# BigBird attention and MLP-mixer on one Trainium2 core: head pairs with row-tiled score matmuls, long row loads, token mixing in half batches, instructions ordered by hand

## The chip, the cores and the metric

The kernel runs on one core of one Trainium2 chip. The time is device time in microseconds (us), the median of the fast runs. Runs that fell in a slower state are left out: one of the kernel before (1022.83 us).

PE is the matmul engine, DVE the vector engine, ACT the scalar engine, POOL the engine that issues the loads here. PSUM tiles are where PE leaves its results; in both kernels the mixer has two of them (the pool named `psM`, tiles named `pm`). QK is the score matmul, PV the product of the exponentials with the values; tok1, tok2, ch1 and ch2 are the four matmul stages of the mixer. A link is a step that the next one must wait for, such as a group of matmuls or the operation that empties its tile. "L362" is line 362 of the kernel in question. "Granted clock" is the share of full speed that PE was given; 0.5 is the half clock. Its record begins with its first change, so the head of the span shows 1.00 even where matmuls took twice as long.

## The reference

Four batches, 8 heads, 768 positions, head size 64. Block-sparse attention (24 blocks of 32, a mask from band, edges and three sampled blocks per row) is followed by an MLP-mixer over the 512 channels:

```python
mask = (np.abs(blk_i - blk_j) <= 1) | first_or_last_block | sampled        # 768 x 768
scores = np.where(mask, q @ k.T / 8, -1e9);  attn = softmax(scores);  x = attn @ v
x = x.transpose(0, 2, 1, 3).reshape(4, 768, 512)
h = np.maximum(x.T @ w_tok1, 0.0) @ w_tok2          # token mixing: 768 -> 256 -> 768
u = x + h.T
out = u + np.maximum(u @ w_ch1, 0.0) @ w_ch2        # channel mixing: 512 -> 1536 -> 512
```

## The kernel before

It computes every score (the mask doesn't save work), transposed: keys on the partitions. One head is a slot; the mask rides in 24 extra rows of the operands, so that one 88-row matmul gives masked scores. The mixer of a batch runs beside the attention of the next. The order is left to a scheduler with priorities.

```python
def qkv_src_ap(t, b, h):                                  # 256-byte pieces (64 floats)
    return APx(t, (b * H + h) * S * D, [[D, 128], [128 * D, NC], [1, D]])
# ... per slot: 6 transposes of q and of k, each 64 wide (qtb, ktb rows 0..63); rows 64..87 hold the mask
for j in range(NC):                                       # NC = 6 key blocks of 128
    ps = psS.tile([128, S], FP32, tag="ps", ...)
    nc.tensor.matmul(out=ps[:, 0:512], lhsT=kt[0:88, 128*j:128*j+128], rhs=qt[0:88, 0:512], ...)
    nc.tensor.matmul(out=ps[:, 512:768], lhsT=kt[0:88, 128*j:128*j+128], rhs=qt[0:88, 512:768], ...)
    nc.scalar.activation(out=et[:, j, :], in_=ps[:, :], func=AF.Exp, scale=0.125)
    for c in range(NC):                                   # PV, 65 columns (64 + the row sum)
        nc.tensor.matmul(out=po[:, c, :], lhsT=et[:, j, 128*c:128*c+128], rhs=vaug[n][:, j, :], ...)
# ... the mixer of a whole batch: 2 groups tok1, 6 tok2 (+ transposes of u), 24 ch1, 6 ch2
# ... every group: matmuls into a pm tile (two of them), then a DVE operation that empties it
```

The softmax here doesn't subtract the row's maximum and nothing guards it: scores larger than these inputs give would overflow.

## Time and profile before

364.21 us in the median, with 2786 matmuls. The prediction below shows the busy table, the stages and the order on PE; what it leaves out is the clock in 40 slices of the span, the DMA packets by size, and two groups of instructions (busy us, mean ns of one, then idle time before them and its cause).

ACT does the exponentials alone, and the mixer's ReLUs lie on DVE.

### The profile page before, as it was taken

The numbers are of one execution on the slowest core, as the hardware profiler recorded it, in microseconds if no ns is written. First come the engines' busy times: TensorE is split into PE (matmuls) and PEld (weight loads), VectorE is DVE, ScalarE is ACT, GpSimd is POOL, SyncE is SP. The second block draws the span as 40 slices with busy tenths as digits, with TensorE's granted clock in tenths as the row PEclk, the third lists the DMA queues.
The fourth block names the chain that finished last, engine by engine and source line by source line (L and its number), as shares of the span: only waits on it lengthen the run. The fifth ranks groups of instructions, "written<-read, shape, count | busy, mean of one in ns | idle before, by whom it ended". The sixth has DMA issues, their size and how long they took to land.

```text
span 362.9 us, 6617 instructions
## 1 busy us (share of the span) xinstructions
PE 325.2 (90%) x2786; PEld 183.3 (51%) x2786; DVE 182.1 (50%) x478; ACT 142.1 (39%) x193; POOL 89.7 (25%) x123
## 2 busy tenths in 40 slices
PE   0795688899899999999999999999999999679995
PEld 0453356565556555455555555455555555235542
DVE  3331243436768633356667544347676534546722
ACT  1293467775622334465604333385404440000000
POOL 9954543524310222233210222220000000000000
PEclk9997599999999999999999999999999999859999
DMA  5999959688641455559531565651101012000022
GB/s 40 136 198 194 153 37 67 46 54 53 41 29 8 28 62 85 84 61 60 33 23 11 34 88 84 75 51 12 13 0 13 2 58 98 21 0 2 0 85 90
DMA packets 82162, 20.24 MB, mean 56 GB/s; under 512 B 75892, under 2 KB 78548, under 8 KB 82132
## 3 DMA queue, kind: packets, MB, share of 16 engines
q0 software_dynamic: 78496, 13.38, 47.3%
q1 hardware_dynamic: 3636, 6.44, 4.7%
q8 instruction: 22, 0.36, 0.4%
q14 instruction: 8, 0.07, 0.1%
HBM read 26.74 MB, written 6.29 MB: 91 GB/s over the span
## 4 chain that ended last, share of the span: by engine, by line
PE 76%; ACT 8%; DMA 8%; POOL 3%; DVE 2%; issue 2%; ACTq 0%; POOLq 0%
PE pm_ch L296 19%; PE pm_ch L313 16%; PE ps L214 13%; PE po L224 10%; ACT et L222 8%; PE ps L218 5%; PE tk L196 4%; DMA w_ch<-in_moe_w_ch_dram 3%; PE pm_tok L249 3%; PE tq L188 3%; PE pm_tok L268 3%; DMA qsrc<-in_q_dram 3%; DMA w_tok<-in_moe_w_tok_dram 2%; PE pm_ut L279 2%; DVE u L276 1%
## 5 line engine op out<-in xcount | busy, mean ns | idle before, releaser
L222 ACT ACTIVATE et<-ps 128x768 bf16<-128x768 f32 x192 | 140.8, 814 | 155.2 <-PE po L224 132.6
L214 PE MATMUL ps<-qtb,ktb 88*128 88x512 bf16 x192 | 76.3, 397 | 7.8 <-ACT et L222 6.4
L296 PE MATMUL pm_ch<-uT,w_ch 128*128 128x384 bf16 x384 | 75.0, 332 | 0.0
L313 PE MATMUL pm_ch<-w_ch,rc 128*128 128x512 bf16 x288 | 71.4, 379 | 0.0
L302 DVE TENSOR_SCALAR rc<-pm_ch 128x384 bf16<-128x384 f32 x96 | 53.1, 556 | 18.3 <-PE pm_ch L296 14.3
L224 PEld LDWEIGHTS <-et 128*128 128x128 bf16 x1152 | 50.7, 100 | 18.0 <-issue 2.8
L224 PE MATMUL po<-vaug,et 128*128 128x65 bf16 x1152 | 58.2, 196 | 0.0
L218 PE MATMUL ps<-qtb,ktb 88*128 88x256 bf16 x192 | 54.2, 282 | 0.0
L132 POOL DMA_DIRECT2D ksrc<-in_k_dram x32 | 26.7, 833 | 96.1 <-PE tk L196 86.0
L296 PEld LDWEIGHTS <-w_ch 128*128 128x128 bf16 x384 | 36.7, 99 | 27.1 <-issue 4.2
L193 DVE COPY qtb<-tq 64x768 bf16<-64x768 bf16 x32 | 17.6, 549 | 61.3 <-PE ps L218 59.7
L134 POOL DMA_DIRECT2D vaug<-in_v_dram x32 | 26.5, 829 | 77.6 <-PE po L224 74.3
L313 PEld LDWEIGHTS <-rc 128*128 128x128 bf16 x288 | 26.5, 97 | 27.5
L234 DVE TENSOR_SCALAR x<-po,recip 128x64 bf16<-128x64 f32 x192 | 39.7, 276 | 1.0
L320 DVE TENSOR_TENSOR o<-pm_ch,u 128x512 f32<-128x512 f32 x24 | 16.5, 687 | 38.7 <-PE pm_ch L313 38.7
L201 DVE COPY ktb<-tk 64x768 bf16<-64x768 bf16 x32 | 17.6, 549 | 34.6 <-PE tk L196 32.5
L218 PEld LDWEIGHTS <-ktb 88*128 88x128 bf16 x192 | 19.0, 99 | 27.3 <-issue 19.3
L133 POOL DMA_DIRECT2D qsrc<-in_q_dram x32 | 26.6, 831 | 8.5 <-PE tq L188 7.8
L214 PEld LDWEIGHTS <-ktb 88*128 88x128 bf16 x192 | 19.0, 99 | 14.1 <-issue 2.8
L188 PE MATMUL tq<-ident,qsrc 128*64 128x128 bf16 x192 | 18.3, 236 | 7.6 <-DMA qsrc<-in_q_dram 5.9
L196 PE MATMUL tk<-ident,ksrc 128*64 128x128 bf16 x192 | 23.0, 234 | 1.1 <-DVE qtb L193 1.1
L196 PEld LDWEIGHTS <-ksrc 128*64 128x64 bf16 x192 | 13.5, 113 | 18.3 <-issue 17.3
(48 smaller groups left out, 127.5 us busy)
## 6 DMA issues: line engine op xcount, KB each, us to landing
out_dram<-o SPq DMA_DIRECT2D x24, 256.0 KB, 2.3
ksrc<-in_k_dram POOLq DMA_DIRECT2D x32, 96.0 KB, 3.1
qsrc<-in_q_dram POOLq DMA_DIRECT2D x32, 96.0 KB, 3.4
vaug<-in_v_dram POOLq DMA_DIRECT2D x32, 96.0 KB, 3.1
w_ch<-in_moe_w_ch_dram POOLq DMA_DIRECT2D x8, 384.0 KB, 11.1
w_tok<-in_moe_w_tok_dram POOLq DMA_DIRECT2D x2, 384.0 KB, 7.3
ktb<-indf SPq DMA_DIRECT2D x2, 36.0 KB
qtb<-e2sb SPq DMA_DIRECT2D x2, 36.0 KB
```

Of the source, the lines that this page charges most:

```text
L132: nc.gpsimd.dma_start(out=ksrc[n][:, :, :], in_=qkv_src_ap(k, b, h))
L133: nc.gpsimd.dma_start(out=qsrc[n][:, :, :], in_=qkv_src_ap(q, b, h))
L188: nc.tensor.matmul(out=tq[:, 128 * c : 128 * c + 128], lhsT=qsrc[n][:, c, :], rhs=ident[:, :], start=(c == 0), stop=(c == NC - 1), is_tran ...
L196: nc.tensor.matmul(out=tk[:, 128 * c : 128 * c + 128], lhsT=ksrc[n][:, c, :], rhs=ident[:, :], start=(c == 0), stop=(c == NC - 1), is_tran ...
L214: nc.tensor.matmul(out=ps[:, 0:512], lhsT=kt[0:88, 128 * j : 128 * j + 128], rhs=qt[0:88, 0:512], start=True, stop=True,)
L218: nc.tensor.matmul(out=ps[:, 512:768], lhsT=kt[0:88, 128 * j : 128 * j + 128], rhs=qt[0:88, 512:768], start=True, stop=True,)
L222: nc.scalar.activation(out=et[:, j, :], in_=ps[:, :], func=AF.Exp, scale=0.125)
L224: nc.tensor.matmul(out=po[:, c, :], lhsT=et[:, j, 128 * c : 128 * c + 128], rhs=vaug[n][:, j, :], start=(j == 0 and c == 0), stop=(j == NC ...
L234: nc.vector.tensor_scalar(out=x_tiles[c][:, 64 * h : 64 * h + 64], in0=po[:, c, 0:64], scalar1=recip[:, c : c + 1], scalar2=None, op0=ALU. ...
L296: nc.tensor.matmul(out=pm[:, 0:384], lhsT=w_ch1[:, dmc, 128 * cc : 128 * cc + 128], rhs=st["uT"][:, dmc, 384 * sh : 384 * sh + 384], start ...
L302: nc.vector.tensor_scalar(out=rc[:, cc, 384 * sh : 384 * sh + 384], in0=pm[:, 0:384], scalar1=0.0, scalar2=None, op0=ALU.max,)
L313: nc.tensor.matmul(out=pm[:, :], lhsT=rc[:, cc, 128 * sc : 128 * sc + 128], rhs=w_ch2[:, cc, :], start=(cc == 0), stop=(cc == 11),)
```

## The change

Its intent, part by part: two heads share the array as row tiles (64 rows each), so that their score matmuls may run side by side; the mask, which has no rows left, comes by a second row-tiled pair of matmuls; positions are permuted so that a partition loads 1.5 KB in one row; token mixing is done in two channel halves, the first as soon as two of the four head pairs of a batch are there; and every engine's order is written by hand, with generators that yield the PE nanoseconds of each matmul. The diff replaces nearly the whole body. Its core:

```diff
-    for j in range(NC):                       # one head, 88 rows, mask included
-        nc.tensor.matmul(out=ps[:, 0:512],   lhsT=kt[0:88, ...], rhs=qt[0:88, 0:512], ...)
-        nc.tensor.matmul(out=ps[:, 512:768], lhsT=kt[0:88, ...], rhs=qt[0:88, 512:768], ...)
+    def qk(s):                                # a head pair, half the queries, one key block
+        for hd in range(2):
+            nc.tensor.matmul(out=ps[:, hd, 0:384],
+                lhsT=kT[p][64*hd:64*hd+64, 128*j:128*j+128],
+                rhs=qT[p][64*hd:64*hd+64, 384*half:384*half+384], start=True, stop=not pe_mask)
+        if pe_mask:
+            for hd in range(2):
+                nc.tensor.matmul(out=ps[:, hd, 0:384], lhsT=ind[64*hd:64*hd+64, j, :],
+                    rhs=e2[64*hd:64*hd+64, 384*half:384*half+384], start=False, stop=True)
+    PE_MASK_BATCHES = (0, 1, 2, 3)            # all; yet mask_full() still builds the other mask
-        nc.vector.tensor_scalar(out=rc[...], in0=pm[:, 0:384], scalar1=0.0, op0=ALU.max)   # ch1
+        relu(eng[sh], rc[...], pm[:, 0:384])  # ("act", "act"), last batch ("act", "dve")
+    def ch2(b):
+        for sc in range(NC):
+            pm = psM.tile(...)
+            for cc in range(12):
+                nc.tensor.matmul(out=pm[:, :], ...)
+                yield 216                     # the order may leave the generator here
+            nc.vector.tensor_tensor(out=o, in0=pm[:, :], in1=u[:, sc, :], op=ALU.add)
+    first, filler = deque(), deque()
+    def run(budget):
+        while spent < budget and (first or filler):
+            work = first or filler            # whatever is in `first` goes before the filler
+            spent += next(work[0])            # (StopIteration: popleft)
+    for n in range(len(steps) + LAG):         # 192 steps
+        ets[n] = qk(steps[n])
+        run(rate / 2)                         # rate = (CH + 2*TOK + 4*TR) / 48 from batch 1 on
+        pv(steps[n - LAG], ...)
+        if half == 1 and j == NC - 1 and p % 2 == 1:
+            first.append(tok(p // 4, (p % 4) // 2, ...))     # a token half
+        run(rate / 2)
```

`filler` holds the channel mixing of the batch before (ch1, ch2); `first` holds the transposes of the next pair and the token halves.

## The prediction

> **What bounds the kernel now.** I read the busy table first, then a table of busy time by stage (stretches cut where the first exponential, the second batch, the last batch and the last mixer's parts begin), then the costliest groups, then the order of time on PE. The busy table names PE; the stages say where PE is the limit and where not. The columns of the second fence are busy us and count of PE, weight loads, DVE, ACT, POOL, then granted clock, DMA share, GB/s.
>
> ```profile
> PE 325.2 (90%) x2786; PEld 183.3 (51%) x2786; DVE 182.1 (50%) x478; ACT 142.1 (39%) x193; POOL 89.7 (25%) x123
> ```
>
> ```profile
> 0.00:15.20 15.20, 4.90 (x29) 3.32 (x30) 5.26 (x16) 1.28 (x1) 14.53 (x30) 1.00 0.98 72
> 15.20:76.80 61.60, 50.46 (x513) 31.38 (x512) 20.73 (x74) 41.08 (x56) 30.30 (x40) 0.89 1.15 114
> 76.80:155.80 79.00, 77.01 (x696) 43.52 (x695) 43.75 (x115) 34.32 (x48) 20.28 (x25) 1.00 0.56 50
> 155.80:235.00 79.20, 77.14 (x696) 43.55 (x696) 44.06 (x115) 34.84 (x48) 19.66 (x24) 1.00 0.52 51
> ...
> 308.40:324.30 15.90, 10.59 (x49) 4.39 (x49) 8.58 (x18) 0.00 (x0) 0.00 (x0) 0.70 0.04 14
> 324.30:343.50 19.20, 19.20 (x98) 9.90 (x96) 13.23 (x24) 0.00 (x0) 0.00 (x0) 0.90 0.00 1
> 343.50:362.90 19.40, 15.60 (x73) 6.85 (x70) 4.71 (x7) 0.00 (x0) 0.00 (x0) 0.99 0.21 82
> ```
>
> The reader is to see four stages. The head is 15.2 us. Batch 0 has attention alone and takes 61.6 us, with PE waiting: on DMA (3.95 us before one query transpose at 32 us, 1.95 at 41.5) with the half clock that followed, and later on ACT. Batches 1 and 2 (attention beside the mixer of the batch before) are PE-bound at 79.1 us each, 97% busy at full clock; batch 3 likewise, 73.4. The tail, the last mixer alone, is 54.5 us; its first 15.9 us is a chain of short PE and DVE steps at a clock that sagged to 0.70.
>
> Busy time of PE doesn't say what a matmul costs, since ends are modelled. What it costs is start to start. The order of time on PE (start, us, line, count):
>
> ```profile
> 128.24 0.38 PE L214 MATMUL ps<-qtb,ktb 88*128 88x512 bf16 x1
> 128.46 0.27 PE L218 MATMUL ps<-qtb,ktb 88*128 88x256 bf16 x1
> 128.56 0.38 PE L313 MATMUL pm_ch<-w_ch,rc 128*128 128x512 bf16 x1
> ...
> 129.84 0.27 PE L218 MATMUL ps<-qtb,ktb 88*128 88x256 bf16 x1
> 130.04 0.41 PE L196 MATMUL tk<-ident,ksrc 128*64 128x128 bf16 x4
> 130.38 0.39 PE L214 MATMUL ps<-qtb,ktb 88*128 88x512 bf16 x1
> ```
>
> 512 columns take 0.22 us and 256 take 0.10 to 0.11 (128.24, 128.46, 128.56), so a column costs 1/2.4 ns and a matmul 2 ns beyond. But 256 columns followed by a transpose with a 64-column stationary (128*64) take 0.20: 95 ns more; and four transposes (4 x 0.055 = 0.22) take 0.34 before the next full-array matmul. Over all pairs of neighbours in this trace at full clock, going into a 128*64 run costs 95 to 97 ns and coming out 98 to 99 ns, while going between full-size operations (QK, PV, both channel matmuls, the 128*128 transposes of u) costs 2 ns.
>
> **What the Trainium skill says.** "TensorEngine Tiling (Array Packing)", section Key Properties: changing the tiling mode, not merely the tile, drains TensorE. The trace agrees, if the 128*64 transposes run as column tiles: about 0.097 us each way. The same section says that different tiles load weights and multiply in parallel; no matmul of the kernel before shows it. "TensorE: Matmul & The Clock Gate", section The HAM clock gate, has the half clock until some 4 us of sustained work; the trace has it until 21 us of the span and again from 31 to 45 us, after the DMA wait. "DMA: Bandwidth & Descriptors", section Why small descriptors are slow: fixed costs per descriptor. The trace agrees: a packet that writes 128 bytes takes 32 ns, one of 1024 takes 98, one of 3072 takes 248.
>
> **The change part by part.** I sum PE time start to start, at full clock.
>
> QK. Before, per 128x768 block of scores: 88 rows, 768 columns, 0.324 us, the mask riding in 24 extra rows for nothing. After, a step is a head pair, half the queries, one key block, again 768 scores per partition, 192 steps. Two matmuls of 64 rows and 384 columns lie on the two row halves; if they run side by side they take 0.162 us. The mask's two matmuls take another 0.162. So row tiling gains a factor of two and the mask gives it back. On top, each step goes from the full array to half-height tiles and back: 0.096 + 0.098, if a row switch costs what the column switch did, and I allow 0.02 to 0.03 for the second tile's start. Sum 0.54 to 0.55 us a step against 0.324: 192 x 0.22 = 42 us more PE work. This is the central number, and the least certain.
>
> Transposes. 384 of 128 columns become 192 full ones: 192 x 0.055 = 10.6 us less. They also no longer switch mode: the trace has 184 changes in and out of them, 184 x 0.097 = 18 us less, of which part lay in batch 0 beside ACT.
>
> PV. 1152 matmuls of 65 columns at 29 ns (27 + 2), 0.175 us a step, unchanged. Token and channel matmuls have the same columns: channels 24 x 4 x 0.162 + 72 x 0.216 = 31.1 us a batch; token half-batches with their transposes 3.3 us each. A full 0/1 mask is also built that no batch uses (all four take the PE mask): 14 matmuls, with switches about 14 x 0.36 = 5 us in batch 0.
>
> ACT. The exponentials have the same size, 0.71 us back to back (six in 4.32), and 72 ReLUs of the channel mixer move from DVE (0.556 us) to ACT. Estimated 0.5 us each: in the ReLU phase 0.71 + 1.3 x 0.5 = 1.4 us a step, beside a PE step of about 1.55. It fits, with little to spare.
>
> DMA. Packets go from 128 to 768 bytes; between the measured 65 ns (512) and 98 (1024) that is some 80 ns for six times the bytes. The queue's stall around 30 to 44 us should go: at the 205 GB/s that the 1024-byte packets moved, pair 4 lands near 37 us and is first needed near 45.
>
> Now by stage.
> - Head. POOL issues three loads first (0.75 to 0.83 us each), then builds identity, indicator (two of memset 0.7 + 0.82 + 0.82) and band: band done near 10.5 us against 7.4 before. In DVE's order the first pair's re-layout stands behind the mask's chain, which waits for the band. Then 0.17 + 0.52 + 0.4, re-layout 3 x 0.3, transposes at half clock 2 x 0.65, two copies 0.55, mask rows 1.3, two casts of 0.94: first exponential near 16.6 us, **1.4 later**.
> - Batch 0: 48 x (0.545 + 0.175) = 34.6, transposes 2.7, unused mask 5, first token half 3.3, its waits 2, cold clock at the start 2.3: 50 us against 61.6, **11.6 less**. PE is above ACT's 48 x 0.71 = 34.
> - Batches 1 to 3: 34.6 + 31.1 + 2 x 3.3 + 2.7 = 75 each, and the waits in the token halves (x to matmul about 0.8, ReLU behind an exponential 0.5, u to transposes 0.9) some 2.2 per half: 79.5 each, 238.5 against 231.6, **7 more**.
> - Tail: half of the token mixing is already done. About 8.5 us to the first channel matmul (before 15.9), 16 for channel 1 at full clock with ReLUs on two engines (before 19.2), 19.4 for the rest: 44 us, **10.5 less**.
>
> 1.4 - 11.6 + 7 - 10.5 = -13.7 us: 350 us. I move it down to 346, as the change's filler budget (841 ns a step) leaves out any drain, which hints that its author saw none as large.
>
> **Rivals.**
> (a) Row switches cost little. Then 192 x 0.19 = 37 us go: about 315. For it: the trace shows only the column kind. Against it: the skill's page makes no difference between the kinds.
> (b) The row halves do not run side by side, or the mask's weights can't be loaded while their half multiplies. The first adds up to 192 x 0.32 = 62 us (about 410), the second up to 0.05 x 192 = 10 us. Nothing in the trace before speaks for or against; the skill's pages speak against the first.
> (c) ACT becomes the bound in the ReLU phase, as PE waits for a pm buffer behind an exponential: 0.2 us a step in 72 steps would be 14 us, about 360. For it: 1.4 of 1.55 us, and only two pm buffers.
> (d) The first loads or DVE's strict order (re-layout waiting for a DMA, everything behind it waiting too) stall batch 0: 5 to 10 us.
>
> **Range and chances.** The sum's largest doubt is the 42 us of QK, with half of it either way in the likely cases; waits and head add some 6 us. That gives 318 to 369. Faster by over 2% means below 357: I give 0.71. Same (to 372) 0.18, slower 0.11, mainly rival (b) or (c).
>
> **What would show it.** In the profile after: the two QK matmuls of a step starting within some 30 ns of each other, and the mask pair 0.16 later (side by side), or 0.16 apart each (rival b); 0.09 to 0.1 us extra before the first QK and after the last mask matmul (drain), or 2 ns (rival a); first exponential at 16 to 17 us; second batch at 65 to 68 us; 79 to 80 us per batch from there; under 5% of waits on ACT; a tail of 43 to 46 us at a clock near 1.0; no long wait on k, q or v loads. The prediction is wrong if the step of QK isn't near 0.54 us, or if PE waits for pm buffers behind ACT.

## More of the kernel before

```profile
PEclk9997599999999999999999999999999999859999
DMA packets 82162, 20.24 MB, mean 56 GB/s; under 512 B 75892, under 2 KB 78548, under 8 KB 82132
L222 ACT ACTIVATE et<-ps 128x768 bf16<-128x768 f32 x192 | 140.8, 814 | 155.2 <-PE po L224 132.6
L302 DVE TENSOR_SCALAR rc<-pm_ch 128x384 bf16<-128x384 f32 x96 | 53.1, 556 | 18.3 <-PE pm_ch L296 14.3
```

PE has the full clock nearly throughout the middle of the span. The transfers are mostly small packets.

## The result, and the profile after

The kernel after took **390.85 us** in the median (390.68 to 392.12), 1.0753 times the kernel before (95% interval 1.0697 to 1.081): slower, and above the predicted range. Here and below a ratio is the mean time of one kernel's fast runs over that of the other's of the same rounds, so it isn't quite the ratio of the medians quoted. All outputs are right.

The page after, busy table, clock and packets:

```profile
PE 333.9 (86%) x3090; PEld 156.6 (40%) x3090; DVE 116.4 (30%) x253; ACT 192.3 (49%) x283; POOL 49.5 (13%) x79
PEclk9985999999999589999999889999999989999999
DMA packets 19171, 20.12 MB, mean 52 GB/s; under 512 B 1348, under 2 KB 15428, under 8 KB 19140
```

PE's busy time went up by 9 us, while the span (389.0 in the profile) went up by 26. The small packets are nearly gone. The clock now has dips where before it had none: in the middle of the span. The stages, cut at the first exponential, at the first exponential of each next batch, and at the begin of the tail (columns as in the prediction):

```profile
0.00:18.80 18.80, 4.22 (x20) 1.53 (x20) 6.25 (x23) 1.28 (x1) 16.66 (x34) 1.00 0.54 70
18.80:72.50 53.70, 50.95 (x564) 23.40 (x565) 25.71 (x58) 37.94 (x49) 18.79 (x27) 0.87 0.91 148
72.50:164.00 91.50, 81.69 (x771) 37.99 (x769) 24.63 (x53) 48.45 (x74) 8.26 (x12) 0.94 0.24 43
164.00:256.00 92.00, 81.08 (x771) 37.63 (x770) 23.94 (x52) 49.02 (x75) 5.79 (x9) 0.96 0.20 38
256.00:345.00 89.00, 78.42 (x765) 36.62 (x763) 21.30 (x44) 49.09 (x75) 0.00 (x0) 0.98 0.06 20
345.00:389.00 44.00, 37.57 (x210) 19.45 (x210) 14.60 (x25) 6.48 (x13) 0.00 (x0) 0.98 0.10 37
```

Against the stages of before that the prediction uses:

| stage | before | predicted | after |
|---|---|---|---|
| head | 15.2 | 16.6 | 18.8 |
| batch 0 | 61.6 | 50 | 53.7 |
| batches 1 to 3 | 231.6 | 238.5 | 272.5 |
| tail | 54.5 | 44 | 44.0 |

The two columns of times aren't cut quite alike: those of before end a batch with its last PV, those of after at the next batch's first exponential, which comes 2.3 us ahead of that. Cut after the last PV as well, the kernel after has 56.0 us in batch 0, 270.6 in the three batches and 43.6 in the tail; no reading below changes.

The tail and batch 0 gained as meant. The three batches in the middle lost 41 us (39 by the second cut), and there the PE is not 97% busy as before, but 81.1 of 92.0 us (88%) in the second of them, at a clock of 0.96. So the question is what PE waits for in the middle.

First the disputed step itself, the order on PE after:

```profile
101.44 0.34 PE L245 MATMUL ps<-qT,kT 64*128 64x384 bf16 x2
101.61 0.33 PE L253 MATMUL ps<-e,ind 64*128 64x384 bf16 x2
101.87 0.66 PE L362 MATMUL pm_ch<-uT,w_ch 128*128 128x384 bf16 x3
102.36 0.34 PE L281 MATMUL po<-vaug,et 128*128 128x65 bf16 x6
```

The two score matmuls are one entry, since they start 3 to 4 ns apart; the mask's pair follows 0.17 us later, and the next full-array matmul 0.26 after that, where 384 columns are 0.16: 0.095 us more. Over all steps at full clock the way into the row tiles and the way out cost about 95 ns each, as much as the column switch did before. A step is thus 0.43 us from its first matmul to the next full-array one, and 0.095 before it: 0.527.

Now the longest wait of the middle. The order on PE, ACT and DVE around the first token half of batch 2, the half in mid-batch (in brackets the idle time before, and what ended it):

```profile
213.64 0.61 PE L375 MATMUL pm_ch<-w_ch,rc 128*128 128x512 bf16 x2
...
218.41 0.59 ACT L307 ACTIVATE a_t<-pm_tok 128x512 bf16<-128x512 f32 x1
219.06 0.60 PE L334 MATMUL pm_tok<-a_t,w_tok 128*128 128x256 bf16 x4 [1.45 <-ACT a_t L307]
219.69 0.69 DVE L339 TENSOR_TENSOR u<-pm_tok,x 128x512 bf16<-128x512 f32 x1 [4.43 <-PE pm_tok L334]
220.44 1.01 PE L334 MATMUL pm_tok<-a_t,w_tok 128*128 128x256 bf16 x4 [0.60 <-DVE u L339]
...
224.02 0.49 PE L346 MATMUL pm_ut<-ident,u 128*128 128x128 bf16 x6 [0.45 <-DVE u L339]
...
226.71 0.68 DVE L381 TENSOR_TENSOR o<-pm_ch,u 128x512 f32<-128x512 f32 x1
```

At 213.64 a group of the channel mixing (ch2) gets its last matmuls. The addition that empties its PSUM tile, `o` at 226.71, stands on DVE behind all of the token half's operations: the group is complete (its twelfth matmul is the second at 213.64), but the generator had yielded after it, `first` took over, and the addition is only emitted when the filler comes back. So one of the mixer's two PSUM tiles holds a finished group for 13 us, and the token half goes through the other alone: four matmuls, wait for DVE, four matmuls, wait for DVE. From 220.44 the matmuls also get longer (1.01 us for the same four): PE has the half clock. This is the same in the mid-batch half of all three batches.

The waits of PE over the span (us in total, how many, the longest) give the sizes:

```profile
PE pm_tok L334 <- ACT a_t L307: 7.9, 6, 1.5
PE tq L228 <- DVE kT L234: 5.2, 8, 0.7
PE pm_ch L362 <- ACT rc L307: 4.4, 18, 0.2
PE pm_tok L334 <- DVE u L339: 2.1, 4, 0.6
```

Summed over batch 2 by start to start, beyond what the columns need: 8.9 us in the links of the two token halves, 2.4 before the query transposes, which wait until DVE has emptied the key transposes' tile (3 of 0.8), 3.3 before ch1 groups (8 of 0.41), and 3.6 us for the lower clock. 75 + 8.9 + 2.4 + 3.3 + 3.6 = 93.2 against 92.0 measured; it is too much since 75 has the QK step at 0.545 us (0.527 gives 74.1), and since some of the time at the lower clock was waiting anyway. The prediction had 75 and 4.4.

In batch 0 the clock is the point. One stretch of batch 0:

```profile
25.80:39.40 13.60, 13.44 (x85) 4.46 (x85) 7.57 (x17) 5.67 (x7) 6.79 (x10) 0.50 1.18 207
```

For 13.6 us, while the mask that no batch uses is built in between, PE ran at the half clock though the profile shows it hardly idle.

### The profile page after: what moved, and what is told of

It is laid out like the page before. It is cut to its first block, busy times and chain, and to the rows that moved or that the text cites. A ratio compares the mean times of both kernels' runs of the same rounds, so it can differ in the third digit from the quotient of the medians.

```text
span 389.0 us, 7139 instructions
## 1 busy us (share of the span) xinstructions
PE 333.9 (86%) x3090; PEld 156.6 (40%) x3090; DVE 116.4 (30%) x253; ACT 192.3 (49%) x283; POOL 49.5 (13%) x79
## 4 chain that ended last, share of the span: by engine, by line
PE 75%; ACT 9%; DVE 8%; POOL 3%; DMA 2%; issue 2%; ACTq 0%; POOLq 0%
PE pm_ch L375 18%; PE pm_ch L362 14%; PE ps L245 13%; PE po L281 9%; PE ps L253 8%; ACT et L260 6%; PE pm_tok L334 4%; PE pm_tok L316 3%; ACT rc L307 2%; DMA w_tok2r<-in_moe_w_tok_dram 2%; DVE u L339 2%; PE pm_ut L346 2%; PE tk L228 2%; PE tq L228 2%; DVE x L293 1%
## 5 line engine op out<-in xcount | busy, mean ns | idle before, releaser
L260 ACT ACTIVATE et<-ps 128x768 bf16<-128x768 f32 x192 | 153.9, 810 | 153.9 <-PE ps L253 151.1
L245 PE MATMUL ps<-qT,kT 64*128 64x384 bf16 x384 | 67.6, 348 | 0.0
L253 PE MATMUL ps<-e,ind 64*128 64x384 bf16 x384 | 66.6, 340 | 0.3 <-DVE e L179 0.3
L307 ACT ACTIVATE rc<-pm_ch 128x384 bf16<-128x384 f32 x84 | 38.7, 489 | 19.6 <-PE pm_ch L362 19.6
L245 PEld LDWEIGHTS <-kT 64*128 64x128 bf16 x384 | 18.8, 93 | 67.6 <-issue 62.6
L375 PEld LDWEIGHTS <-rc 128*128 128x128 bf16 x288 | 20.9, 99 | 25.7 <-issue 17.1
L334 PE MATMUL pm_tok<-a_t,w_tok 128*128 128x256 bf16 x96 | 17.8, 301 | 11.5 <-ACT a_t L307 7.9
L339 DVE TENSOR_TENSOR u<-pm_tok,x 128x512 bf16<-128x512 f32 x24 | 16.3, 691 | 35.3 <-PE pm_tok L334 35.2
L316 PE MATMUL pm_tok<-x,w_tok 128*128 128x256 bf16 x96 | 16.8, 274 | 3.9 <-DVE x L293 3.9
L253 PEld LDWEIGHTS <-ind 64*128 64x128 bf16 x384 | 19.4, 97 | 0.0
L293 DVE TENSOR_TENSOR x<-po,recip 128x384 bf16<-128x384 f32 x32 | 17.8, 558 | 1.1
L334 PEld LDWEIGHTS <-w_tok 128*128 128x128 bf16 x96 | 9.4, 102 | 18.6 <-issue 16.6
## 6 DMA issues: line engine op xcount, KB each, us to landing
w_ch<-in_moe_w_ch_dram POOLq DMA_DIRECT2D x8, 384.0 KB, 10.1
```

What stands on the lines that cost most here:

```text
L245: nc.tensor.matmul(out=ps[:, hd, 0:384], lhsT=kT[p][64 * hd : 64 * hd + 64, 128 * j : 128 * j + 128], rhs=qT[p][64 * hd : 64 * hd + 64, 38 ...
L253: nc.tensor.matmul(out=ps[:, hd, 0:384], lhsT=ind[64 * hd : 64 * hd + 64, j, :], rhs=e2[64 * hd : 64 * hd + 64, 384 * half : 384 * half + ...
L260: nc.scalar.activation(out=et[:, :, :], in_=ps[:, :, 0:384], func=AF.Exp, scale=0.125)
L293: nc.vector.tensor_tensor(out=free(xs[b][:, 3 * half, 128 * pb : 128 * pb + 128], 0, [[64, 2], [DM, 3], [1, 64]]), in0=po[:, :, :, 0:64], ...
L307: nc.scalar.activation(out=o, in_=i, func=AF.Relu)
L316: nc.tensor.matmul(out=pm[:, t, :], lhsT=w_tok1[:, sc, 128 * t : 128 * t + 128], rhs=x[:, sc, 256 * g : 256 * g + 256], start=(t == 0 and ...
```

## The experiments

Each kernel is the one after with one part undone or added, unless the text says otherwise. In the expectations, A is the theory that I held, and the other letters are its rivals; each says what it would give. Times are medians. The ratio is to the kernel before of the same chip; the kernel before lay between 360.0 and 368.5 us in all of its fast runs, so that a difference of 2 us between experiments of different chips means nothing.

| run | what it is | us | ratio to before (95%) |
|---|---|---|---|
| after | | 390.85 | 1.075 (1.070–1.081) |
| e1 | unused mask not built | 379.83 | 1.044 (1.036–1.053) |
| e2 | `first` only between filler groups | 376.27 | 1.036 (1.028–1.044) |
| e3 | mask by DVE in batches 1 to 3 | 366.49 | 1.009 (0.996–1.022) |
| e4 | full-height QK instead of row tiling | 373.73 | 1.030 (1.019–1.040) |
| e5 | ch1 ReLUs on DVE | 380.44 | 1.050 (1.041–1.059) |
| e6 | 256-byte loads | 396.81 | 1.094 (1.085–1.104) |
| e7 | links spaced by filler | 370.37 | 1.027 (1.013–1.041) |
| e8 | e4 + e1 + e7, ReLUs on both engines | 339.36 | 0.935 (0.927–0.943) |
| e9 | e8 with row tiling again | 358.59 | 0.991 (0.983–0.999) |
| e10 | whole-batch token mixing | 362.89 | 1.005 (0.993–1.017) |
| e11 | QK of two steps together | 391.54 | 1.085 (1.076–1.093) |
| e12 | e8, 7% less filler per step | **335.81** | **0.929** (0.925–0.933) |
| e13 | both token halves at the batch's end | 371.03 | 1.025 (1.018–1.032) |
| e14 | e10 + e4 + e1, ReLUs on both engines | 341.41 | 0.944 (0.936–0.952) |
| e15 | e14 with row tiling again | 352.96 | 0.976 (0.969–0.982) |
| e16 | e9 + e11 | 348.50 | 0.952 (0.946–0.958) |
| e17 | e12 with whole-batch token mixing | 354.44 | 0.969 (0.960–0.978) |

### Parts of batch 0: the unused mask (e1) and the loads (e6)

```diff
-                    filler.append(mask_full())
```

> Undo only the building of the full 0/1 mask that no batch uses (14 matmuls of 24 rows and 14 evacuations in the first two pairs). Theory A (the change's QK cost was predicted right, the missing 40 us are waits in the hand order and the half clock that they bring): the first pair's 12 steps took 20.8 us at half clock against 10 for the second pair; without the mask the clock should stay full from about 24 us on and the start of batch 1 should come 8 to 11 us earlier: 380 to 383 us. Rival (the half clock comes from the start itself, not from these matmuls): only their own time goes, 3 to 5 us: 386 to 388 us.

379.83 us, 11.0 less than after. Batch 0 goes from 53.7 to 43.8 us, the other stages by less than 4 us. The 14 matmuls with their switches are 5 us by the prediction's own count; the other half is the clock, as the same stretch of e1 shows:

```profile
22.00:39.00 17.00, 17.00 (x228) 8.31 (x228) 6.77 (x16) 15.95 (x22) 9.07 (x13) 1.00 1.21 206
```

228 matmuls in 17 us, at full clock but for the first 1.8 us (by the lengths of the matmuls), where after had 85 at half clock in 13.6.

```diff
-   raw[:, :, :, :] <- APx(t, 2*p*S*D, [[NC*D, 128], [S*D, 2], [1, NC*D]])         # 1.5 KB rows
+   for hd: raw[:, hd] <- APx(t, (2*p+hd)*S*D, [[D, 128], [128*D, NC], [1, D]])      # 256 B
```

(The patterns of the indicator, the token weights and the output follow the old order of positions.)

> Undo only the 1.5 KB row loads: queries, keys and values come in 256-byte pieces again, one transfer per head, with the token order of the kernel before. If loads are hidden either way, 389 to 393 us; if the queue's stall that the kernel before had at 28 to 44 us comes back (75,000 packets instead of 19,000), batch 0 becomes 5 to 10 us longer: 396 to 401 us. My theory says the second, since pairs are needed faster in batch 0 than heads were.

396.81 us, 6.0 more than after: the first exponential comes at 21.6 us instead of 18.8, and batch 0 takes 56.6 instead of 53.7. The profiled execution was its fastest, 394.1, with batch 1 at 88.5 instead of 91.5: that batch had no half clock in e6, and 10.2 us of it in after. So the long rows are worth 3 to 6 us, and they are earned by the end of batch 0.

### The token halves in mid-batch (e2, e7, e10, e13)

e2 lets `first` begin only where no channel group is between its first matmul and its emptying:

```diff
+    held = [False]            # ch1, ch2: True after pm is taken, False (and yield 0) after it is emptied
-            work = first or filler
+            work = filler if held[0] and filler else first or filler
```

> Undo the interruption in mid-group: token halves and transposes may start only when the channel mixer's current group has been evacuated, so that they have both pm buffers, not one. Theory A: a token half is a chain of PE, evacuation, PE on a single buffer, because the interrupted group holds the other; its waits (6 to 7 us a half with the half clock, 8 halves, and the transposes' 0.8 us each) should fall by a third to a half: 15 to 25 us less, 366 to 376 us. Rival B (the waits are the chain's own dependencies, matmul to ReLU to matmul to add to transpose, and the second buffer changes nothing): 388 to 392 us.

376.27 us, 14.6 less. The token half of batch 2 on PE in e2:

```profile
213.98 0.60 PE L334 MATMUL pm_tok<-a_t,w_tok 128*128 128x256 bf16 x4 [1.45 <-ACT a_t L307]
214.41 0.34 PE L281 MATMUL po<-vaug,et 128*128 128x65 bf16 x6
214.59 0.60 PE L334 MATMUL pm_tok<-a_t,w_tok 128*128 128x256 bf16 x4
...
215.56 0.61 PE L334 MATMUL pm_tok<-a_t,w_tok 128*128 128x256 bf16 x4
```

With two tiles the three groups follow each other without a wait, 1.6 us from the first to the third where after took 3.2, and the clock is 1.0 throughout batches 1 to 3 (85.5, 86.6 and 84.0 us, together 16 less than after). What stays is the wait for ACT ahead of them. Breaking into open groups, which is all that e2 forbids, is thereby shown to cost some 15 us, clock included.

e7 puts 0.7 us of filler between the links of the chains in `first`, if the filler is ready, and carries what was overspent into the next step:

```diff
+        yield None        # in tok and transposes, after each operation that the next link waits for
+            if r is None: state["gap"] = 700; continue        # ns of filler before the next link
```

> Keep every operation of the change and alter the hand order alone: after each step of a token half or transpose pair that PE must wait for (x, ReLU, add, copy), some 0.7 us of channel-mixer matmuls are put in before the next, and the filler's budget is carried over from step to step, not started afresh. Theory A (waits in the token halves and the half clock they bring make most of the missing 33 us of batches 1 to 3): these waits, about 11 us a batch, and 1.5 to 5 us a batch of half clock should mostly go: 358 to 370 us. Rival (the time is PE's own, QK with its switches and masks): 385 us or more.

370.37 us, 20.5 less, at a clock of 1.0 in batches 1 to 3: at the upper end of the expected range. That gains only 6 us more than e2. A reason, argued and not shown: a first token half has filler of the batch before between its links, while the last half has none until the channel mixing that waits for it may begin.

e13 leaves the halves as they are but starts both after the batch's last pair; e10 makes one chain of them, with 512 columns:

```diff
-            if half == 1 and j == NC - 1 and p % 2 == 1:
-                first.append(tok(p // 4, (p % 4) // 2, "act" if p >= 4 else "dve"))
+            if half == 1 and j == NC - 1 and p % 4 == 3:
+                for g in range(2):                                    # e13
+                    first.append(tok(p // 4, g, "act" if p >= 4 else "dve"))
+                first.append(tok(p // 4, "act" if p >= 4 else "dve"))  # e10 instead: whole batch
```

> Undo only the half-batch token mixing: one token part of 512 columns after the last head pair of a batch. There is then one chain of 2 ReLUs, 6 adds and 4 copies a batch, where there were two of 1, 3 and 2. Theory A: the waits per link stay (about 0.7 us for 12 links a batch either way), batches 1 to 3 change by under 5 us, and the tail gets the first half back, 3.3 us of matmuls and 4 to 5 us of waits: 393 to 402 us. Rival (the halves themselves are what made batches 1 to 3 long): under 385 us.

> Keep the halves of token mixing as they are, but start the first half with the second, after the last head pair of the batch. Then no token half is put into the middle of a channel-2 group that holds one of the two pm buffers. If the place in mid-batch is what costs (and the single buffer left there), this gains nearly what the full-batch form gained: 363 to 370 us. If it is the halves' shorter chains of 256 columns, wherever they stand: 382 us or more.

e10 took 362.89 us, 28 less than after and even with the kernel before. This contradicted theory A of that time, which had it unchanged or slower: the chain is as long, and yet the time falls. e13, made to tell place from size, took 371.03, just above its range for the place: about 20 of the 28 us come from taking the first half out of mid-batch. The rest isn't cleanly that of longer matmuls and fewer links: 5.2 us of it lie in batch 0 (44.8 us in e10, 50.0 in e13), where by the lengths of the matmuls e10 ran 7 us at half clock and e13 22.7, with the same mask being built. Batch 2 of e10:

```profile
146.60:229.70 83.10, 76.29 (x739) 33.94 (x745) 23.82 (x52) 48.88 (x75) 5.76 (x9) 1.00 0.21 42
```

83.1 us at full clock against 92.0 at 0.96. The tail of e10 is longer, 48.6 us against 44.8 (from the last exponential): what the halves save there is 4 us, and they cost 28 + 4 = 32 before it, up to 5 of which are the half clock in batch 0 (7 us of it against 17.2 in after).

### The ReLUs (e5)

```diff
-                    filler.append(ch1(b, ("act", "act") if b < B - 1 else ("act", "dve")))
+                    filler.append(ch1(b, ("dve", "dve") if b < B - 1 else ("act", "dve")))
```

> Undo only the move of the channel mixer's ReLUs to ACT for the first three batches (84 of 96 ReLUs ran on ACT, 486 ns each; DVE took 557). Rival C (ACT, which does an exponential of 810 ns and about 1.5 ReLUs a step, holds back the pm buffers; in the trace PE waits 3.3 us a batch between channel-1 groups): 10 us less, 379 to 382 us. Theory A (these waits are a small part, the token halves' are the large one): 385 to 391 us.

380.44 us, 10.4 less, and PE's wait for ReLUs on ACT before ch1 groups is gone from the trace. PE's waits behind ACT are real, rival (c) of the prediction at three quarters of its size; theory A of that time (385 us or more) was wrong. The group in after:

```profile
L307 ACT ACTIVATE rc<-pm_ch 128x384 bf16<-128x384 f32 x84 | 38.7, 489 | 19.6 <-PE pm_ch L362 19.6
```

One ReLU takes 0.489 us on ACT and 0.556 on DVE, so the operation isn't dearer; it stands in the queue behind an exponential of 0.81.

### Row tiling and its switches (e3, e4, e11)

e3 takes the mask's matmuls from batches 1 to 3 and lets DVE multiply the 0/1 mask in (`PE_MASK_BATCHES = (0,)`).

> Undo the second row-tiled matmul for batches 1 to 3: the mask is multiplied in by DVE after the exponential (batch 0 keeps the matmul, since the full mask is being built then). PE loses 144 x 0.162 = 23 us. Theory A (PE is the bound from batch 1 on and its waits don't change): 367 to 370 us. Rival C (DVE, busy 30%, gets 144 multiplications of about 0.45 to 0.8 us in its strict order and delays the evacuations that PE waits for): 375 to 395 us.

366.49 us, 24 less. 144 steps by 0.162 us are 23.3. The profiled execution was slow, so its stages aren't compared.

e4 undoes the row tiling: two operand tiles per head of 128 rows, in which the other head's 64 rows hold the indicator and the mask rows, so that one full-height matmul of 384 columns per head gives masked scores.

```diff
-                lhsT=kT[p][64*hd:64*hd+64, 128*j:128*j+128], rhs=qT[p][64*hd:64*hd+64, 384*half:...],
-                start=True, stop=not pe_mask)            # and the mask's pair
+                lhsT=kT[p][hd][:, 128*j:128*j+128],      rhs=qT[p][hd][:, 384*half:...],
+                start=True, stop=True)                   # copies of q and k: two per tile, not one
```

> Undo row tiling with everything else kept: each head of a pair gets its own 128-row operands, in which the other head's rows hold the mask's factors or zeros, so QK and mask are one full-height matmul of 384 columns per head and the array never changes its tiling. The trace of the changed kernel gives 0.54 us a step for QK and mask with both switches; this form should take 2 x 0.162 = 0.324. Theory A: 192 x 0.216 = 41 us less, less about 3 us for four more operand copies at the head and two more PSUM copies a pair: 350 to 355 us. Rival D (ACT or the token halves' waits take the freed time): 365 to 380 us.

373.73 us, 17.1 less, where PE work of 192 × (0.527 − 0.324) = 39 us was removed (42 with the prediction's 0.545). It is the rival's outcome: the bulk isn't had. In e4 the QK pair takes 0.32 us from start to start, as before the change, so the work is gone; two waits of e4 show a part of where the time went:

```profile
PE tq L237 <- DVE kh L245: 9.8, 8, 1.2
PE pm_ch L364 <- ACT rc L309: 7.9, 21, 0.6
```

The transposes' wait, 5.2 us in after, is 9.8, and the ReLUs' wait went from 4.4 to 7.9. PE, done sooner, stands before the same links. These two are 8 of the some 22 us; 2.5 more went into the head, whose first exponential comes at 21.3 us instead of 18.8, behind four more operand copies. Batch 0 gained 3.6 us of the 10 removed there; the rest isn't divided.

e11 puts the QK groups of two steps together, which halves the switches: 96 × 0.19 = 18 us of PE time.

```diff
-            ets[n] = qk(steps[n])
+            if n % 2 == 0:
+                ets[n], ets[n + 1] = qk(steps[n]), qk(steps[n + 1])
```

> Keep the change and emit the QK groups of two steps back to back, so that the array changes its tiling 192 times instead of 384. Nothing else is altered. If a switch costs the 95 to 98 ns that the trace shows, 192 x 0.097 = 18.6 us go: 370 to 376 us, provided that the waits don't grow. If switches were hidden by something else: 386 us or more.

391.54 us: nothing. The waits of e11:

```profile
PE pm_ch L362 <- ACT rc L307: 11.2, 18, 0.6
PE pm_tok L334 <- ACT a_t L307: 9.8, 6, 1.8
PE pm_tok L334 <- DVE u L339: 5.0, 10, 0.8
```

11.2 against 4.4, 9.8 against 7.9, 5.0 against 2.1: 11.6 us of the 18 are there as waits on the mixer's links, and two exponentials in a row now stand before a ReLU. Batches 1 to 3 also had 34 us of half clock in this profile, against 20.4 in after, which is up to 6.8 us more. Taken alone e11 could mean that switches are free in practice. e16 below says that they aren't.

### Together (e8, e9, e12, e14 to e17)

e8 joins full-height QK (e4), no unused mask (e1), spaced links (e7) and ch1 ReLUs alternating between ACT and DVE, `("act", "dve")`. e9 is e8 with row tiling and the mask's matmuls again. e12 is e8 with `rate = 0.93 * (...)`, which leaves channel matmuls over to run between the links of a batch's second token half.

> All that helped put together: one full-height QK matmul per head with the mask in the spare rows, no unused mask, the spaced order, channel-1 ReLUs alternating between ACT and DVE. PE work is then 192 x (0.324 + 0.175) + 3 x (31.1 + 6.6) + 4 x 2.7 + head and tail = 96 + 113 + 11 + 20 + 44 = 284 us; batch 0 is bound by ACT at 0.72 to 0.81 us a step (about 38 us, 10 above PE's). Theory A: 298 to 315 us, below both kernels. Rival (ACT's order or DVE's gives the waits back as in the full-height run, where 24 of 41 us were given back): 325 to 345 us.

> The combination of e8 (339.4 us) with row tiling put back: QK as two half-height matmuls and the mask as two more, everything else (spaced order, no unused mask, ReLUs on both engines) as in e8. It measures what row tiling costs when the order no longer hides or returns the difference. By the trace's 0.216 us a step, in batches 1 to 3 alone (batch 0 is bound by ACT's 0.72 to 0.81 us a step, against 0.715 of PE): 144 x 0.216 = 31 us more, 366 to 373 us. Rival (most of it is hidden, as in e4 where only 17 us of 41 came through): 352 to 358 us.

> e8 with the filler's rate at 0.93 of its value, so that channel matmuls are left over to cover the second token half of a batch, which in e8 runs with nothing beside it at the start of the next batch. If those uncovered waits (about 5 us a batch) are what is left to gain, 327 to 334 us; if not, 337 to 342 us.

e8 took 339.36 us, a miss of my theory (298 to 315) and within the rival's range: PE is left waiting in all three batches (78.0, 77.9 and 75.1 us, where the columns alone, without row tiling, need 75 − 48 × 0.22 = 64). e9 took 358.59, less than the 366 to 373 expected, so row tiling costs 19.2 us there (39 us of work, 31 expected), net of the 2.5 us by which the head of the full-height form is longer. e12 took **335.81 us**, between the two ranges given for it, and is the fastest of all: 7.1% less than before. It keeps the change's head pairs, long rows and token halves and an order by hand (spaced), and drops its row tiling. Its busy line and its batch 2:

```profile
PE 280.1 (84%) x2672; PEld 175.9 (53%) x2692; DVE 148.9 (45%) x315; ACT 176.6 (53%) x247; POOL 49.2 (15%) x79
135.70:211.10 75.40, 65.14 (x658) 41.74 (x661) 33.73 (x71) 44.63 (x62) 5.58 (x8) 1.00 0.22 40
```

PE is busy 65.1 of 75.4 us. No engine is at its limit; what is left is still waiting in chains.

e14 takes another way to the same end: the plain order of after with whole-batch token mixing (e10), full-height QK, no unused mask and both engines for ReLUs. e15 is e14 with row tiling again. e16 is e9 with QK in twos. e17 is e12 with whole-batch token mixing.

> Token mixing by the whole batch, full-height QK with the mask in the spare rows, no unused mask, channel-1 ReLUs on both engines; the order of the change otherwise (no spacing). If the gains of e10 (28 us), e4 (17) and half of e1 and e5 (about 10 together) add: 335 to 340 us; if PE is then really the bound, its work of 284 us and the waits of the full-batch chain (5 us a batch) would give 325 to 332 us.

> The same with row tiling and the mask's own matmuls put back. It measures row tiling a second time, in another order than e9. If the 19 us of e9 over e8 hold: e14 + 17 to 24 us. If PE is the bound all through batches 1 to 3: e14 + 31 us.

> e9 (row tiling in the spaced order, 358.6 us) with the QK groups of two steps back to back, so half the tiling switches. In e11 the same edit on the changed kernel gave nothing, and PE's waits for channel-1 ReLUs grew. If switches cost time once PE waits less: 96 switches of 0.097 us fewer in batches 2 to 4 and as many more in batch 1: 10 to 18 us less, 341 to 349 us. If two exponentials in a row again hold back what follows: 355 us or more.

> e12 (335.8 us) with whole-batch token mixing in place of halves, and the spacing kept. e14 against e8 says that halves and whole batch are even once nothing is interrupted in mid-group (341.4 and 339.4 us), so no large difference is expected: 328 to 338 us.

e14: 341.41, near e8 without any spacing. e15: 352.96, so that row tiling costs 11.5 us in this order (17 to 24 or 31 expected: a miss), and a kernel with the row tiling kept is 2.4% faster than before; the tiling alone isn't what made the change slower. e16: 348.50, 10.1 less than e9. The same edit gave nothing in e11 and 10 us here, after the waits were thinned out: the switches cost time once PE is what the step waits for. e17 missed: 354.44 against 328 to 338. Its tail is 67.6 us, 13.7 of them at half clock, against 52.3 in e12, with only 12 PE instructions more. Its edit didn't keep the spacing: filler may run before and after the six tok2 groups of the whole batch, but no longer after each. The trace shows the fault of the kernel after once more: a ch2 group gets its last four matmuls at 289.81 us and is emptied (`o`) at 300.04, and meanwhile the tok2 groups go one by one through the other tile and wait 0.78 us each for DVE.

## Why the prediction was wrong

The mechanism on PE was right, the sum was not. By its own steps:

- **The QK step, "0.54 to 0.55 us a step against 0.324: 192 x 0.22 = 42 us more PE work"**: nearly right in the trace: 0.527 (0.17 from the QK pair to the mask's, about 0.095 per switch, row halves 3 to 4 ns apart), so 39 us. Rivals (a) and (b) are out. But it was carried into the time one to one, and in the time it was worth 17.1 us (e4), 19.2 (e9 less e8) and 11.5 (e15 less e14).
- **Head, "first exponential near 16.6 us"**: 18.8, 2.2 us more. The band was done at 12.05 us and not "near 10.5", and the second cast (0.95 us) wasn't hidden: on PE the second pair of mask-row matmuls waits for DVE's cast of the first, and the first scores for the second cast.
- **Batch 0, "50 us"**: 53.7. The unused mask, "5 us", was 11 (e1), since the clock halved while it was built.
- **Batches 1 to 3, "some 2.2 per half: 79.5 each, 238.5"**: this is the step that failed; they took 272.5, 34 more. I took the waits of a token half as three short ones: 0.8 for `x`, 0.5 for the ReLU, 0.9 for `u`. In the first half of batch 2 they are 0.55, 1.45, and 0.45, 0.65 and 0.65 for `u` and its transposes, and 0.60 that I didn't have at all: between one tok2 group and the next. The trace of batch 2 has 8.9 us in its two halves' links, 5.7 before transposes and ch1 groups, and 3.6 of lost clock. The largest cause is shown by e2: the half begins between the last matmul of a channel group and the operation that empties it, which leaves it one PSUM tile (15 us over the kernel). It could be read from the order of instructions of the changed kernel, which I had: `o` of the open group is emitted after the half. With e2 the three batches still take 256, 18 over the prediction; the ReLUs' 10 us (e5) may be among them, the rest isn't divided. e13 confirms the place with 20 us; e10's 28 have part of batch 0's clock in them.
- **Rival (c)**, ACT before the ReLUs, "14 us": 10 (e5). I had given it as an alternative; it came on top.
- **Tail, "44 us"**: 44.0, in part by luck: 6.8 us to the first channel matmul (8.5 predicted), 17.4 for channel 1 (16), 19.8 for the rest (19.4). **Loads**: no long wait, and worth 3 to 6 us (e6).
- **"I move it down to 346, as the change's filler budget leaves out any drain"**: a guess at the author's knowledge, and in the wrong direction. The budget adds up the filler's own matmuls, so it says nothing of drains in QK.

Off the sum of 350: 2.2 + 3.7 + 34 = 40, which with it is 390. The parts measured one by one (11, 15 to 28, 17, 10) overlap and are not to be added; e14 with four of them has 49 us less than after.

What stays open: why the clock halves in batch 0 while PE is shown busy. With the same mask matmuls it had 17.2 us of half clock there in after, 7 in e10 and 22.7 in e13, by the lengths of the matmuls; without them (e1) 5. Open too is how the rest of e12's waits, 7 to 10 us a batch, divides.

## What to carry to other kernels

When work is interleaved by hand, break off only where no PSUM tile holds a finished but unemptied result, and check it in the order of instructions: for each tile, is the operation that empties it emitted before the other chain begins? A saving or a cost in PE work counts in the time only as far as PE doesn't wait for short links in the same stretch, so price the links first, and test a removal again after the waits are gone. A chain of matmul, emptying, matmul needs independent work between its links, and early work (here half the token mixing) gains only what its later place would have exposed: 4 us here, for some 27 to 32 paid.

## What the Trainium skill lacked or had wrong

- "TensorEngine Tiling (Array Packing)", section Key Properties, says that a change of tiling mode drains TensorE, but gives no size: about 95 ns each way here, for row tiles (64 rows) as for column tiles (64 columns), and 192 steps with two of them each are 37 us of PE time.
- "TensorE: Matmul & The Clock Gate", Part 3, section The mechanism, says in its list that a weight load overlaps with running matmuls only when the row group differs, though its first paragraph allows the background weight buffer too. Here the "only" is wrong: the mask's weights go to the same two row halves, and their load is recorded from 217.12 us, while the QK pair of 217.10 runs; the mask's pair starts some 10 ns after the 160 ns of the QK pair.
- The same page, section What's actually happening, gives the full clock after some 3.4 us of sustained work. The kernel after has 13.6 us at the half clock with PE shown busy for 13.44 of them. The section A second HAM failure mode: psum-queue depth-cycling has short waits between matmul groups bring the half clock, but no length of them. The mid-batch token half fits it: a mean clock of 0.81 from 216 to 228.5 us, where the half clock came at 220.3 after a single wait of 1.45 us and the start of one of 0.60. In e2, where the second tile is free, the same 1.45 us brought none, and batches 1 to 3 have 1.00 throughout.
- No page has it that a PSUM tile can be held by a finished group because the order of emission puts its emptying behind another chain (15 us, e2), nor that PE time taken away may come back as waits (0 us in e11, 10 us in e16 for the same edit).
